# A linear-attention and token-mixing kernel: state kept as diagonal blocks, V loaded by whole batches, token sums on column halves, and a new order of steps

## The chip, the cores and the metric

The kernel runs on one core of a Trainium2 chip. The metric is device time in microseconds, as a median over executions. A core has five engines with queues of their own: TensorE (PE), VectorE (DVE), ScalarE (ACT), GpSimd (POOL) and SyncE (SP), which here issues almost all of the DMAs. [...]

## The reference

There are 4 batches, 8 heads, 768 tokens and 48 columns per head. The first part is a recurrence over the tokens; the second mixes tokens with a low rank and ends in a projection:

```python
for t in range(S):
    cur = einsum('bhd,bhe->bhde', u[None] * kt, vt)
    y[:, :, t] = einsum('bhd,bhde->bhe', rt, state + cur)
    state = wt[:, :, :, None] * state + einsum('bhd,bhe->bhde', kt, vt)
...
x = y.transpose(0, 2, 1, 3).reshape(B, S, H * D)          # 768 x 384 per batch
W_tok = scale * einsum('bsd,btd->bst', x @ w_q, x @ w_k)   # 64 columns each
out = maximum(einsum('bst,btd->bsd', W_tok, x), 0) @ w_out
```

Inputs and output are float32.

## The kernel before

**Tiling.** The work is cut into 12 units of 256 tokens, three to a batch, and each unit into two chunks of 128 tokens. Token pairs lie side by side in a row of a load, so each plain load moves runs of 384 bytes. The heads lie in four pairs; the two heads of a pair take 48 rows each of the two 64-row halves of the 128 partitions.

**A unit.** `load` brings w, k, r and v (one DMA each of 384 KB; tiles wg, kg, rg, vg, four buffers each). The logarithm of w (`f_ln`, tile lw) is summed over tokens by matmuls (`f_cw`), and `f_en`, `f_ep` take exponentials of both signs (tiles en, ep). K and R are cast to bf16 (`f_c16`, L475), transposed on TensorE (`f_rawT`), and multiplied with the exponentials: RT (`f_RT`, L536) and KT (`f_KT`, L547). Scores are matmuls of KT and RT with 48-row weights (`f_A`), masked on VectorE into AM (`f_am`, L619). The product of r, k and u gives one number per token and head (`f_dps`, `f_dd`), which scales V into Vd (`f_vd`, L601).

**State.** KT is transposed back (`f_kb`) and copied as kd (`f_kd`). In `f_sn` the outer products of kd and V are made by pairs of heads, so that 96 x 96 blocks hold the two heads' states on the diagonal and unused products beside it; four pairs make 384 columns. The state carried on is added by a matmul with an identity. `f_sb` (L666) decays it on VectorE by the tile ptm, which GpSimd makes (`f_ptm`) from ep and MB; MB holds zeros that clear the blocks off the diagonal. `f_y` adds, for one chunk, eight matmuls of AM and V and four of RT and the state SB.

**V.** For seven of the twelve units (`DIRECT`) `load_v` (L226) brings V with four DMAs of 192-byte runs to the rows in which it is needed, and one cast makes VB. For the other five a plain load is cast (tile v16), and `f_vp` moves its rows by matmuls with PM.

**The second part.** `f_x` (L707) makes X from y and Vd; `f_xt`, `f_qk` make the two projections (tile QK). After the third unit of a batch, `f_T` sums over all tokens of the batch: six matmuls of 384 columns, whose 128 weight columns are the 64 of a chunk and the 64 beside them; `f_Ts` copies 64 rows into a tile TS whose other rows are zero. Then per unit `f_mx`, `f_rl` (tile MX), `f_fp` and `f_os` make the output rows (tile os), and a DMA stores them.

**Order.** A planner (`Plan.order`) merges five queues, one per engine. The place of each step in its queue is written out in `RANK`; the engine of a step that could run on several is in `ENG`. The planner walks the queues with assumed durations and gives PSUM banks as it goes. [...] The 51 matmuls of zeros (tile Z) keep TensorE busy: nine at the start, 26 after the first unit's sums, 16 marked for the end.

**Set-up.** Before the first step VectorE clears the double buffers lw, r16, k16, kd, ts whole, GpSimd makes masks and identities (CM, PM, ID16, US), and ScalarE loads u.

Of the kernel before, what the change touches and what calls it, by code (L numbers as in the profile page):

```python
# [14 lines left out]
AX = mybir.AxisListType  # L15
# [9 lines left out]

class Plan:

    def __init__(self, kinds, switch):
        self.kinds = kinds
        self.switch = switch
        self.steps = []

    def add(self, eng, dur, rank, fn, after=(), fill=None, read=(), lag=100, mode=0,
            behind=None):
        s = dict(mode=mode, behind=behind, eng=eng, dur=dur, rank=rank, fn=fn, after=[a for a in after if a is not None],  # L40
                 fill=fill, lag=lag, n=len(self.steps), out=[])
        s["buf"] = None if fill is None else dict(readers=[])
        self.steps.append(s)
        for a in read:
            self.reads(s, a)
        return s

    def dma(self, issue, dur, rank, fn, after=(), fill=None, read=()):

        i = self.add("SP", issue, rank, fn, after, fill, read, lag=0)  # L50
        m = self.add("DQ", dur, 0, self.nothing, [i], lag=0)
        return i, self.add(f"L{m['n']}", 1950, 0, self.nothing, [m], lag=0)

    def nothing(self):
        pass

    def reads(self, s, a, own=False):

        if not own:
            s["after"].append(a)  # L60
        if a["buf"] is not None:
            a["buf"]["readers"].append(s)

    def order(self):
        never = 1 << 60
        queues = {e: [] for e in ("PE", "ACT", "DVE", "POOL", "SP")}
        for s in sorted(self.steps, key=lambda s: s["rank"]):
            if s["eng"] in queues:
                queues[s["eng"]].append(s)
            for a in s["after"]:  # L70
                a["out"].append(s)
        free = dict.fromkeys(queues, 0)
        free["DQ"] = 0
        place = dict.fromkeys(queues, 0)
        rings, owners, moved, done, mode = {}, [None] * 8, [], [], 0

        def clear(buf):

            if buf is None:
                return 0  # L80
            return max([x.get("end", never) for x in buf["readers"]], default=0)

        def start(s):

            if any("end" not in a for a in s["after"]):
                return never, None
            if s["behind"] is not None and "start" not in s["behind"]:
                return never, None
            t = max([free[s["eng"]]] + [a["end"] for a in s["after"]])
            if s["behind"] is not None:  # L90
                t = max(t, s["behind"]["start"])
            if s["eng"] == "SP" and len(moved) >= 3:
                t = max(t, moved[-3])
# [13 lines left out]
            if s["fill"] is not None:  # L107

                ring, size = rings.setdefault(s["fill"], []), self.kinds[s["fill"]]
# [9 lines left out]
        while True:  # L119
# [7 lines left out]
            if at is not None:  # L127
                s["buf"]["bank"] = at
# [4 lines left out]
            change = e == "PE" and s["mode"] != mode  # L133
            if e == "PE":
                mode = s["mode"]
            run(s, t, s["dur"] + self.switch * change)
            if e == "SP":
                for m in s["out"]:
                    if m["eng"] == "DQ":
                        run(m, max(free["DQ"], s["end"]), m["dur"])  # L140
                        moved.append(free["DQ"])
                        for x in m["out"]:
                            if x["eng"].startswith("L"):
                                run(x, m["end"], x["dur"])
        assert len(done) == len(self.steps)
        return done


@with_exitstack
def kernel(  # L150
# [24 lines left out]
    HW = H * D2  # L175

    SHIFT = 25
    MU = -SHIFT * math.log(2.0) / C

    def mm(o, l, rr, start=True, stop=True, trans=False):  # L180
        nc.tensor.matmul(o, l, rr, start=start, stop=stop,  # L181
                         skip_group_check=True, is_transpose=trans)
# [4 lines left out]
    sm = ctx.enter_context(tc.tile_pool(name="sm", bufs=3))  # L187
    bt = ctx.enter_context(tc.tile_pool(name="bt", bufs=2))
# [6 lines left out]
    NB = 4  # L195
    WG = [const([C, HW], F32, f"wg{i}") for i in range(NB)]
    RG = [const([C, HW], F32, f"rg{i}") for i in range(NB)]
    KG = [const([C, HW], F32, f"kg{i}") for i in range(NB)]
    VG = [const([C, HW], F32, f"vg{i}") for i in range(NB)]
    NOS = 4  # L200
    OS = [const([C, 2 * DM], F32, f"os{i}") for i in range(NOS)]
    EW = 132

    KDS = [const([C, 1024], BF16, f"kd{i}") for i in range(2)]
    LW = [const([C, 2 * H * 64], BF16, f"lw{i}") for i in range(2)]
    R16 = [const([C, 2 * H * 64], BF16, f"r16{i}") for i in range(2)]
    K16 = [const([C, 2 * H * 64], BF16, f"k16{i}") for i in range(2)]
    QK = [const([C, NU * 384], BF16, f"qk{i}") for i in range(2)]
    TS = [const([C, DM], BF16, f"ts{i}") for i in range(2)]
    EP = [const([C, 8 * EW], BF16, f"ep{i}") for i in range(2)]  # L210

# [8 lines left out]

    def load_v(b, i, tl):

        for c in range(2):
# [693 lines left out]
```

## Time and profile before

| what | us |
|---|---|
| median of three executions | 108.14 (107.78 to 108.36) |
| the profiled execution: span, first to last instruction | 105.2 |
| the profiled execution's own time | not on the page; the three executions lie 2.6 to 3.2 above the span |
| busy: PE / DVE / ACT / POOL | 96.2 / 88.1 / 79.9 / 71.0 |
| moved by DMA | 24.62 MB, 58,896 of 61,217 packets under 512 bytes |
| last load landed, last store landed | 82.30, 104.15 |

The granted TensorE clock is 1.000 in the whole span. A busy PE is modelled: its matmuls overlap, so the steps from start to start say more than its busy time. A line of a group reads: line, engine, operation, output <- inputs, shapes, count, then busy us and mean ns, then the idle time of the engine just before it. All matmuls go through one helper at L181, so they are told apart by their tiles.

### The profile page before, as it was taken

Reading aid. Unit: us, or ns where it says so; the run is one execution under the profiler, and the core shown is the slowest. Engines: PE = TensorE matmul, PEld = TensorE weight load, DVE = VectorE, ACT = ScalarE, POOL = GpSimd, SP = SyncE. Lnnn points to the kernel's source line nnn. Section 1 sums busy time; section 2 is a strip of 40 time slices with the busy share of each in tenths; the row PEclk is TensorE's granted clock in tenths of the full one; section 3 lists DMA queues with packets and bytes.
Section 4 is the critical chain, followed back from the end, with each engine's and each line's share of the span. In section 5 each row is a group of like instructions: output and inputs, shape, how many; then the busy total and the mean of one; then the engine's idle time right before and its main releaser. Section 6 shows DMA issues by size and latency. Waiting matters only on the chain.

```text
span 105.2 us, 3714 instructions
## 1 busy us (share of the span) xinstructions
PE 96.2 (91%) x1506; PEld 70.2 (67%) x1506; DVE 88.1 (84%) x138; ACT 79.9 (76%) x123; POOL 71.0 (67%) x92
## 2 busy tenths in 40 slices
PE   5969889997999998999997897779999999998995
PEld 2246566686887786968796775658697987856551
DVE  6898997898999999798999996786998889754740
ACT  4367778797989868997899959867898895954610
POOL 6600859599997996979979993968689699000000
DMA  1999999999999898989997969998997870033564
GB/s 28 298 324 325 325 323 270 238 297 175 312 316 264 148 272 230 288 172 310 325 311 142 213 123 269 350 289 209 288 255 143 303 307 18 0 153 150 199 243 160
DMA packets 61217, 24.62 MB, mean 234 GB/s; under 512 B 58896, under 2 KB 60048, under 8 KB 61200
## 3 DMA queue, kind: packets, MB, share of 16 engines
q1 hardware_dynamic: 60640, 24.19, 85.5%
q10 hardware_dynamic: 560, 0.20, 0.7%
q8 instruction: 11, 0.18, 0.7%
q14 instruction: 6, 0.05, 0.1%
HBM read 19.66 MB, written 4.72 MB: 232 GB/s over the span
## 4 chain that ended last, share of the span: by engine, by line
PE 51%; DVE 14%; DMA 13%; issue 7%; POOL 5%; ACT 4%; SPq 4%; DVEq 0%; ACTq 0%; POOLq 0%
PE PS L181 51%; DMA wg<-in_w_dram 7%; DMA kg<-in_k_dram 6%; SPq L226 3%; DVE SB L666 2%; DVE RT L536 2%; POOL KT L547 2%; DVE qT L529 2%; DVE KT L547 2%; POOL Vd L601 1%; ACT MX L381 1%; SPq L230 1%; ACT kd L373 1%; DVE X L707 1%; DVE kd L265 1%
## 5 line engine op out<-in xcount | busy, mean ns | idle before, releaser
L619 DVE TENSOR_TENSOR AM<-PS,US 128x1024 bf16<-128x1024 f32 x24 | 28.9, 1220 | 1.1 <-PE PS L181 0.7
L547 POOL TENSOR_TENSOR KT<-ks,en 128x1024 bf16<-128x1024 bf16 (+1 forms) x10 | 19.3, 1934 | 1.2 <-ACT en L498 0.6
L601 POOL TENSOR_TENSOR Vd<-VB,dd 128x768 bf16<-128x768 bf16 (+1 forms) x14 | 18.4, 1318 | 2.2 <-ACT dd L371 1.3
L181 PE MATMUL PS<-Z 128*128 128x512 bf16 x51 | 16.2, 424 | 1.5 <-DVE uT L248 1.2
L707 DVE SCALAR_TENSOR_TENSOR X<-PS,gx,Vd 128x768 bf16<-128x768 f32 (+1 forms) x13 | 12.3, 955 | 3.3 <-PE PS L181 2.8
L181 PEld LDWEIGHTS <-KT 48*128 48x128 bf16 (+1 forms) x272 | 10.7, 95 | 6.3 <-issue 3.8
L467 ACT ACTIVATE lw<-wg 128x768 bf16<-128x768 f32 x12 | 10.0, 846 | 5.5 <-DMA wg<-in_w_dram 5.1
L181 PE MATMUL PS<-wo,MX 128*128 128x384 bf16 x72 | 13.5, 326 | 0.1
L504 ACT ACTIVATE ep<-PS 128x1024 bf16<-128x1024 f32 (+1 forms) x14 | 12.7, 922 | 0.9 <-PE PS L181 0.9
L498 ACT ACTIVATE en<-PS 128x1024 bf16<-128x1024 f32 (+1 forms) x14 | 12.5, 904 | 0.5 <-issue 0.3
L666 DVE TENSOR_TENSOR SB<-PS,ptm 128x384 bf16<-128x384 f32 x20 | 11.1, 553 | 1.5 <-PE PS L181 1.3
L181 PE MATMUL PS<-RT,KT 48*128 48x128 bf16 x192 | 9.2, 217 | 1.4 <-POOL KT L547 0.5
L381 ACT ACTIVATE MX<-PS 128x768 bf16<-128x768 f32 (+1 forms) x12 | 8.7, 730 | 1.8 <-PE PS L181 1.7
L475 POOL CAST r<-rg 128x768 bf16<-128x768 f32 x10 | 8.7, 870 | 1.6 <-DMA rg<-in_r_dram 1.5
L475 POOL CAST k<-kg 128x768 bf16<-128x768 f32 x9 | 7.4, 825 | 3.3 <-DMA kg<-in_k_dram 2.0
L181 PE MATMUL PS<-ID,k 128*128 128x128 bf16 x96 | 7.4, 220 | 2.2 <-POOL k L475 1.4
L181 PEld LDWEIGHTS <-MX 128*128 128x128 bf16 x72 | 6.7, 98 | 3.9 <-issue 0.3
L373 ACT ACTIVATE kd<-PS,gv 128x384 bf16<-128x384 bf16 (+1 forms) x11 | 8.1, 740 | 1.4 <-PE PS L181 1.3
L181 PEld LDWEIGHTS <-Z 128*128 128x128 bf16 x51 | 5.0, 105 | 6.0 <-issue 2.3
L371 ACT COPY os<-PS 128x768 f32<-128x768 f32 (+1 forms) x10 | 7.1, 708 | 2.5 <-PE PS L181 2.2
L536 DVE TENSOR_TENSOR RT<-PS,ep 128x1024 bf16<-128x1024 bf16 (+1 forms) x14 | 8.4, 609 | 0.5 <-PE PS L181 0.2
L181 PE MATMUL PS<-CM,lw 64*128 64x128 bf16 x192 | 7.8, 223 | 1.1 <-ACT XT L371 0.7
(82 smaller groups left out, 211.4 us busy)
## 6 DMA issues: line engine op xcount, KB each, us to landing
wg<-in_w_dram SPq DMA_DIRECT2D x12, 384.0 KB, 5.3
kg<-in_k_dram SPq DMA_DIRECT2D x12, 384.0 KB, 5.0
rg<-in_r_dram SPq DMA_DIRECT2D x12, 384.0 KB, 5.1
out_dram<-os SPq DMA_DIRECT2D x9, 384.0 KB, 4.3
vg<-in_v_dram SPq DMA_DIRECT2D x28, 96.0 KB, 3.7
vg<-in_v_dram SPq DMA_DIRECT2D x5, 384.0 KB, 5.0
out_dram<-os SPq DMA_DIRECT2D x5, 192.0 KB, 2.0
wof<-in_moe_w_out_dram SPq DMA_DIRECT2D x1, 576.0 KB, 5.7
```

The source lines that it names most:

```text
L181: nc.tensor.matmul(o, l, rr, start=start, stop=stop, skip_group_check=True, is_transpose=trans)
L381: nc.scalar.activation(o, i, ACT.Relu)
L467: nc.scalar.activation(view(lw, 0, [[64, H], [512, 2], [1, D]]), view(wg, 0, [[D2, H], [D, 2], [1, D]]), ACT.Ln, bias=0.0, scale=math.exp( ...
L475: op(view(dst, 0, [[64, H], [512, 2], [1, D]]), view(src, 0, [[D2, H], [D, 2], [1, D]]))
L498: nc.scalar.activation(sb("en", [C, 1024])[:, cols(cs, 512)], t["cw"][:, cols(cs, 512)], ACT.Exp, bias=0.0, scale=-1.0)
L504: nc.scalar.activation(view(ep, cs[0] * NP * EW + 66, [[EW, NP * len(cs)], [-65, 2], [1, 64]]), t["cw"][:, cols(cs, 512)], ACT.Exp, bias=0 ...
L536: nc.vector.tensor_tensor(view(sb("RT", [C, 1024]), cs[0] * 512, [[C, n4], [64, 2], [1, 64]]), view(t["rT"], cs[0] * 512, [[C, n4], [64, 2 ...
L547: e.tensor_tensor(sb("KT", [C, 1024])[:, cols(cs, 512)], t["ks"][:, cols(cs, 512)], t["en"][:, cols(cs, 512)], ALU.mult)
L601: nc.gpsimd.tensor_tensor(sb("Vd", [C, 2 * DM])[:, cols(cs, DM)], t["VB"][:, cols(cs, DM)], view(t["dd"], cs[0] * H, [[1, len(cs) * H], [0 ...
L619: nc.vector.tensor_tensor(view(sb(f"AM{c}", [C, 1024]), 0, [[C, 8], [1, C]]), view(t[f"A{c}"], 0, [[C, 8], [1, C]]), view(US, 0, [[0, 8], ...
L666: nc.vector.tensor_tensor(view(x, 0, [[D, H], [1, D]]), view(t[f"sn{c}"], 0, [[D, H], [1, D]]), view(t["ptm"], c * 8, [[1, 8], [0, D]]), A ...
L707: nc.vector.scalar_tensor_tensor(view(X["t"], (2 * i + c0) * DM, [[DM, ncs], [1, DM]]), view(t["y"], c0 * 512, [[512, ncs], [1, DM]]), gx, ...
```

## The change

**State.** The state of the four pairs is kept in 192 columns: head 0 of a pair in rows 0 to 47, head 1 in rows 64 to 111, both in the same 48 columns. kd is laid out with a stride of 128 columns between zeros, so that a 128-column slice of it holds one head's columns at the right rows and zeros elsewhere. `f_sn` makes one matmul of 48 columns per head, and adds the carried state by a matmul with IDU, an identity scaled by 2 to the power -25; kd is scaled by the same number (gk). SB is decayed by ep directly; ptm and MB are gone.

**y.** Its part from the state comes first (`f_yi`), as matmuls with 48-row weights, one per head, in two sides; a side takes one head of a pair from chunk 0 and the other from chunk 1, and a drain of TensorE stands between the sides. The part from AM (`f_ya`) follows.

**V.** For batches 1 to 3 `load_whole` brings the V of the whole batch with four DMAs of 64 rows and 24 runs of 192 bytes per row, into two new buffers vw. VB is cast from it on GpSimd. Batch 0 uses plain loads and `f_vp`.

**Token sums.** In `f_T` chunk 0 of a unit goes to rows 0 to 63 of the PSUM tile and chunk 1 to rows 64 to 127, with 64 weight columns each; TS is copied with all 128 rows.

**Set-up.** Only the 16 pad columns of each 64 are cleared in lw, k16, r16; ts needs nothing; kd is cleared by GpSimd (2,112 columns, twice). The r cast of unit 0 goes to GpSimd.

**Order.** `RANK` is new, `ALT` picks the engine where there is a choice, and 17 movable matmuls of zeros all stand early. The order of the loads and stores on SyncE is new as well.

```diff
-    def load_v(b, i, tl):
-        for c in range(2):
-            src = v[b, :, ds(i * U + c * C, C)].rearrange("h (q j) d -> j q h d", j=2)
-            for j in range(2):
-                nc.sync.dma_start(out=view(tl, c * DM, [[D, H], [1, D]], p0=64 * j, pn=64),
-                                  in_=src[j])
+    def load_whole(b, q, tl):
+        n_ = H // 2 * NCH
+        for j in range(2):
+            nc.sync.dma_start(
+                out=view(tl, q * n_ * D, [[D, n_], [1, D]], p0=64 * j, pn=64),
+                in_=dataclasses.replace(v, offset=(b * H * S + j) * D + q * n_ * C * D,
+                                        ap=[[D2, 64], [C * D, n_], [1, D]]))
...
-    for t in R16 + K16 + KDS:
-        nc.vector.memset(t, 0.0)
+        for x in (tiles["lw"][0], tiles["k16"][0], tiles["r16"][0]):
+            nc.vector.memset(view(x, D, pads), 0.0)
...
+        for x in tiles["kd"]:
+            nc.gpsimd.memset(x, 0.0)
...
-                        mm(x[:, ds(0, DM)], ID16, old.tile, start=True, stop=False)
+                    mm(x[:, ds(0, NP * D)], IDU, old.tile, start=True, stop=False)
...
-                        mm(x[:, ds(hp * D2, D2)], KDS[n % 2][:, ds((c * NP + hp) * C, C)],
-                           t["VB"][:, ds(c * DM + hp * D2, D2)],
+                        mm(x[:, ds(hp * D, D)],
+                           kd.tile[:, ds(64 + (c * H + h) * 128 - 64 * hh, 128)],
+                           VB.tile[:, ds(c * DM + h * D, D)],
...
-                    nc.vector.tensor_tensor(view(x, 0, [[D, H], [1, D]]),
-                                            view(t[f"sn{c}"], 0, [[D, H], [1, D]]),
-                                            view(t["ptm"], c * 8, [[1, 8], [0, D]]), ALU.mult)
+                    view(SB.tile, 0, [[D, NP], [1, D]]), view(at(sn), 0, [[D, NP], [1, D]]),
+                    view(ep.tile, c * NP * EW + 64, [[EW, NP], [0, D]]), ALU.mult),
...
-                    for hp in range(NP):
-                        mm(y[:, ds(c * 512 + hp * D2, D2)], t["RT"][:, ds((c * NP + hp) * C, C)],
-                           old.tile[:, ds(hp * D2, D2)], start=False, stop=True)
+                if not first:
+                    nc.tensor.drain()
+                for hp in range(NP):
+                    for c, hh in side:
+                        mm(of(c, 2 * hp + hh), RT.tile[ds(hh * 64, D), ds((c * NP + hp) * C, C)],
+                           olds[c].tile[ds(hh * 64, D), ds(hp * D, D)],
+                           start=(first and hp == 0), stop=False)
...
-                    mm(batch["T"][:, ds(0, DM)], batch["QK"][:, ds(ii * 384 + c * DH, C)],
-                       X["t"][:, ds(gi_ * DM, DM)], start=(gi_ == 0), stop=(gi_ == NCH - 1))
+                mm(at(T)[ds(c * DH, DH), ds(0, DM)], QK.tile[:, ds(ii * QS + U + c * DH, DH)],
+                   X.tile[:, ds(gi * DM, DM)], start=(gi < 2), stop=(gi >= NCH - 2))
```

## The prediction

> **What bounds the kernel now.** I read the page's engine shares first, then busy time by stage, then the chain of waits, then the table of waits.
>
> ```profile
> PE 96.2 (91%) x1506; PEld 70.2 (67%) x1506; DVE 88.1 (84%) x138; ACT 79.9 (76%) x123; POOL 71.0 (67%) x92
> ```
>
> No engine stands alone, so the stages are asked (columns: stretch, length, busy us of PE, PEld, DVE, ACT, POOL, clock, DMA share, GB/s):
>
> ```profile
> 0.00:10.00 10.00, 7.94 (x55) 3.67 (x57) 7.98 (x27) 5.62 (x10) 3.53 (x20) 1.00 0.90 239
> 10.00:35.00 25.00, 23.34 (x421) 17.53 (x417) 23.29 (x32) 21.33 (x32) 20.67 (x24) 1.00 1.07 276
> 35.00:55.00 20.00, 19.49 (x348) 15.49 (x346) 18.38 (x26) 17.11 (x25) 17.80 (x19) 1.00 1.03 262
> 55.00:70.00 15.00, 12.42 (x239) 9.83 (x236) 12.96 (x18) 12.90 (x19) 12.08 (x13) 1.00 0.92 231
> 70.00:92.50 22.50, 21.96 (x383) 17.65 (x384) 19.87 (x28) 18.55 (x30) 16.89 (x19) 1.00 0.68 195
> 92.50:105.00 12.50, 11.00 (x76) 6.07 (x73) 5.57 (x11) 4.40 (x11) 0.00 (x0) 1.00 0.47 178
> ```
>
> Here is to be seen: from 10 to 35 us VectorE is 93% busy (PE's time there is padded with warm-up matmuls on Z); from 35 to 55 and from 70 to 92.5 TensorE is 97 to 98% busy; from 55 to 70 it loses 2.6 us while nobody is full. What holds it there is in the chain, in order of time:
>
> ```profile
> 59.09 1.58 SPq L226
> 60.72 0.72 SPq L226
> 61.48 0.62 SPq L230
> 62.22 0.58 SPq L230
> 63.30 6.31 DMA kg<-in_k_dram
> 69.66 0.84 POOL k L475
> 70.54 22.65 PE PS L181 x390
> ```
>
> SyncE issues two direct V loads of four DMAs each (L226), the K loads behind them go out late, and the cast of K starts when its load has landed. By the landing times, most loads of the kernel are used within 0.05 to 1.6 us of landing: they are just in time. From 70.5 us on the chain is TensorE without a break until 93 us. At the head, VectorE's memsets (groups of DVE until 8 us) run until 7.16 us, while unit 0's K landed at 5.92:
>
> ```profile
> L265 DVE MEMSET r<- 128x512 uint32 x2 | 1.0, 485 | 0.1
> L265 DVE MEMSET k<- 128x512 uint32 x2 | 1.0, 485 | 0.1
> L265 DVE MEMSET kd<- 128x512 uint32 x2 | 1.0, 485 | 0.1
> ```
>
> [...] a score matmul (48-row weights, 128 columns) that ends its group is followed after 148 ns, where 56 is the step inside a group, and the group before it pays the like (205 instead of 109, 139 instead of 42): some 95 ns each way. [...] 162 ns at 384 columns, 42 at 96, 25 at 48. [...] the half KT on VectorE took 0.43 us with GpSimd idle and 1.05 us beside a GpSimd cast. [...]
>
> **The change part by part.**
>
> *Head.* Off VectorE go 8 memsets of 485 ns (3.88), 2 of 218 for ts (0.44), 3 of 60 for MB (0.18) and the r cast (0.56). Added are 6 memsets of 128 words, 165 each by PM's row (1.0), IDU (0.11 to 0.28 by the rows of ID's memset and US) and gk (0.06). Net -3.8 us, so the k cast can start when K has landed: 1.24 us earlier. But GpSimd gets two memsets of 2,112 columns and the r cast (0.87). No row shows such a memset: at the price per column of GpSimd's cast (825/768 = 1.07 ns) it takes 2.26 us, at half of that, if two values go at once, 1.1. I take 2.0. GpSimd is free of its selects at 4.6, so r is cast by 4.6 + 4.0 + 0.19 (UB) + 0.87 = 9.7; transposes 0.67, RT 0.42, scores 0.40, and the first AM starts at 11.2 instead of 11.99: **-0.8** (-2.6 where the r load's landing at 6.98 binds, +0.2 at 2.26 a memset[...]).
>
> *State.* SB handles 192 columns instead of 384. From 1220 ns at 1024 and 553 at 384 columns the step is 1.04 ns, so 353: 20 times -0.20 = -4.0 us of VectorE. ptm goes from GpSimd (10 x 0.216 + 4 x 0.244 = -3.1). TensorE: outer products 80 x 42 become 160 x 25 (+0.6); the carried state 16 x (82 - 162) = -1.3; the part of y from the state 80 x 42 becomes 160 matmuls in 48-row tiles, 14 ns each if they pair as the scores do (3 ns, then one step), 25 if not: -1.1 to +0.6.
>
> *Token sums and V.* T: 24 x 162 becomes 12 pairs on column halves: -1.9 if they run together, 0 if not. Two fewer repack steps vp: 8 x 81 = -0.65, with two VB copies fewer on ScalarE (-1.6). VB for whole V is GpSimd's cast as before (9 + 3 instead of 7 + 5 casts of 0.82).
>
> *What TensorE pays.* Counted in the two instruction orders, it changes mode 83 times instead of 56: 27 x 0.095 = +2.6. The 13 drains between the two sides of y are not in this trace: 0 (the mode change covers it) to 158 ns (a 48-column matmul's 183 less its 25), I take 100: +1.3. TensorE's sum: +0.6 - 1.3 - 1.0 - 1.9 - 0.65 + 2.6 + 1.3 = -0.35, between -1.8 and +4.0. It is the whole of what is bound by TensorE, at 42.5 of 105 us: **-0.2**.
>
> *Order and engines.* By counts times rows VectorE loses 5.1 us in all, ScalarE 4.9, GpSimd (KT: one full and one half more, +3.3; ptm -3.1) nothing outside the set-up. From 10 to 35 us VectorE sheds KT of units 0, 1 and 3 (2.6, half of unit 0 stays on it) and 0.2 for each of 6 SB, and takes two ks (1.4), a cast (0.56) and a kd (0.4): -1.4. GpSimd takes those KTs and is then full: by its own durations without idle time KT of unit 4 ends at 31.7 instead of 34.5. I take **-0.9** (-2.5 to +1.5).
>
> *Loads.* V in 192-byte runs goes from 7 to 9 units: by packet times 4,096 x 16.7 ns less 2,048 x 22.8, over 16 engines, +1.4 us of transfer. But SyncE issues 12 large V DMAs instead of 28 small of 0.63 us, and a whole V (batch 2's after unit 7's loads, batch 3's after unit 10's) finds a buffer that was freed long before, where a V of one unit now waits for GpSimd's casts. Unit 11's K and W come last, behind two stores; by ScalarE's order and durations the second store's copy is done at 57 us without idle time, some 63 with its present share, so they land near 70, before 72.67 and 73.86 of now. The weights move behind six loads and V: some 38 instead of 25 us, ahead of their first use. I take **-2.3** of the 2.6 lost at 55 to 70 us (-2.6 to +1). ScalarE's gain lies under its 5.1 us of waiting for W: 0. What is late next is GpSimd: its VB of unit 3 waits for the first whole V, due near 34 us (20 loads by 27.4, then 6 to 7.5), and casts, Vd and the weights queue behind; TensorE's y of unit 3 waits for it.
>
> *Tail.* From the end of the last X (92.42) to its last output matmul (100.84) TensorE has 6.9 us of matmuls for 8.4 us; two output blocks of batch 2 (0.98 each) now lie there to fill the rest: **-0.5**. The 15 warm-ups that go from the end cost nothing: the last ended at 104.07, and the last store landed at 104.15.
>
> Sum: -0.8 - 0.2 - 0.9 - 2.3 - 0.5 = -4.7, so a span of 100.5 against 105.2. The median of the runs shown is 108.14, 2.9 above this span (the page gives no other time of the profiled execution); I carry the 2.9 over: **103.4 us**.
>
> **The rivals.**
>
> *Loads set the pace (17%).* For it: slacks of 0.1 us after landing and a DMA share near 1 until 80 us. Against it: 7 us or so of its time are gaps in which SyncE waited for buffers. Then +1.4 stays, the head gives 0.8 and the tail 0.5 back: 108.2.
>
> *TensorE becomes slower (15%).* Its place is y and T: mode changes at 95 ns each, 13 drains at 158, no pairing in y, no pairing in T: +4.0 in the sum above, all of it on the path where engines are as closely matched as from 35 to 92 us, and the order's gain at 55 to 70 us goes to it. 108.14 + 4.0 - 0.8 - 0.5 = 110.8. It decides from the point where TensorE's sum is above +4.5, or above +2.2 if the loads give nothing. For it: 97 to 98% in two stages. Against it: the scores do pair.
>
> *The order fits better than the sum says (10%).* GpSimd, never idle, would end its last Vd at 78.6 instead of 89.5; if three quarters of these 10.9 us reach the end, the span is 97.0 and the time 99.9.
>
> *The forecast (58%)*: 101.0 to 106.2.
>
> **How the numbers follow.** About 0.5% is what a measurement of this kernel can tell from no change: 107.6 to 108.7. Faster holds the forecast, the last case and a fifth of the loads case, less 2%: 0.70. The same: half of the loads case and the forecast's edge: 0.10. Slower: the rest, 0.20. The range runs from 100.0 to 109.0: half of the last case and most of the slow one lie outside.
>
> **What will show it.** Right: first AM near 11.2 us; SB at 353 ns; GpSimd's kd memsets near 2 us; y's state part with steps of 3 and about 25 ns; T in 12 steps of 162; the wait for K near 63 us gone; VectorE's sum near 83. Wrong: GpSimd waiting at VB of unit 3 for more than 3 us; TensorE's idle time between 35 and 92 us above today's; a last K or W landing after 74 us.

## The result, and the profile after

The changed kernel takes **113.39 us** (median of four, 112.17 to 114.45); the kernel before, beside it, 107.96. The ratio is **1.0485 [1.0376, 1.0595]**: slower by about 5 us, where 103.4 us with a range of 100.0 to 109.0 was predicted. A time is the median of all executions, while a ratio leaves out the slow ones of both kernels, so that the two do not divide exactly. The profiled execution is the longest of the four: 114.45 us, at a span of 112.7.

First the shares of the engines, from the page of the changed kernel:

```profile
PE 93.3 (83%) x1633; PEld 69.8 (62%) x1633; DVE 85.2 (76%) x138; ACT 76.1 (68%) x114; POOL 74.8 (66%) x82
```

TensorE, VectorE and ScalarE are all busy for less time than before (96.2, 88.1, 79.9), and the span is 7.5 us longer. For TensorE that is the matmuls of zeros: they take 16.2 us of its busy time before and 8.9 now, so its own work rose from 80.0 to 84.4 us. No engine became the bound of the whole; all of them wait more. By stage (stretch, length, busy us of PE, PEld, DVE, ACT, POOL, granted clock, DMA share, GB/s), still of the changed kernel:

```profile
0.00:10.00 10.00, 7.16 (x40) 2.71 (x40) 5.10 (x20) 5.21 (x9) 8.16 (x23) 1.00 0.91 238
10.00:35.00 25.00, 21.38 (x406) 16.43 (x407) 22.54 (x32) 18.25 (x23) 21.49 (x19) 0.93 1.10 260
35.00:55.00 20.00, 17.19 (x355) 14.14 (x356) 15.82 (x25) 14.61 (x23) 14.30 (x14) 0.91 1.05 252
55.00:70.00 15.00, 12.69 (x236) 9.89 (x235) 11.33 (x18) 10.80 (x15) 11.40 (x12) 1.00 0.93 233
70.00:92.50 22.50, 19.88 (x397) 15.76 (x396) 18.41 (x27) 17.39 (x27) 17.37 (x15) 1.00 0.71 162
```

From 35 to 92.5 us TensorE is busy for 49.8 us; before it was 53.9 in the same stretches. The one column that stays near 1 until 70 us is the DMA share. The chain of waits of the changed kernel says the same (start, length, what):

```profile
32.08 5.78 DMA vw0x<-in_v_dram
...
38.41 0.83 POOL VB1x L543
...
52.10 6.83 DMA vw1x<-in_v_dram
...
59.80 0.83 POOL VB1x L543
...
67.92 0.93 SPq L291
68.91 1.09 SPq L298
...
73.53 5.74 DMA vw0x<-in_v_dram
79.53 0.67 issue
80.20 2.12 POOL KT0x L532
...
84.40 0.83 POOL k161x L458
...
96.30 11.54 PE PS L239 x122
```

Where before had K and then TensorE, there are now three whole V (L298), one for each batch from 1 to 3, with steps of GpSimd behind each: its cast VB after the first two, KT after the third. The table of GpSimd's waits in the changed kernel (us in total, times, longest) has them on top:

```profile
POOL VB1x L543 <- DMA vw0x<-in_v_dram: 6.0, 2, 3.5
POOL r160x L458 <- DMA rg0x<-in_r_dram: 2.4, 2, 1.8
...
POOL k161x L458 <- DMA kg3x<-in_k_dram: 2.1, 2, 1.3
```

It is tempting to stop here: "GpSimd waits for V". The experiments show that taking most of this wait away gains nothing. What the changed kernel loses, and where, can be seen in the units' progress. The start of each unit's X (us), read from the traces; the last two rows are kernels of the experiments:

| unit | 0 | 1 | 2 | 3 | 4 | 5 | 6 | 7 | 8 | 9 | 10 | 11 |
|---|---|---|---|---|---|---|---|---|---|---|---|---|
| before | 18.0 | 24.1 | 30.1 | 38.3 | 44.7 | 55.3 | 60.0 | 67.6 | 73.3 | 82.5 | 86.7 | 91.3 |
| changed | 23.7 | 28.8 | 32.3 | 44.4 | 51.5 | 56.3 | 65.5 | 72.5 | 77.3 | 90.2 | 94.9 | 97.1 |
| a_replan | 15.8 | 23.6 | 32.6 | 41.5 | 47.4 | 52.7 | 63.5 | 71.4 | 75.7 | 85.1 | 92.8 | 93.7 |
| a_replan_m2 | 18.7 | 23.5 | 30.9 | 37.4 | 45.7 | 52.1 | 59.8 | 63.6 | 70.8 | 80.7 | 86.0 | 89.4 |

And the landings, where the changed kernel's loads fall behind (us; from the DMA issues in the traces):

| | W, unit 8 | W, unit 9 | W, unit 11 | K, unit 11 | last input |
|---|---|---|---|---|---|
| before | 54.8 | 55.9 | 72.7 | 73.9 | 82.3 (V, unit 11) |
| changed | 60.6 | 69.0 | 85.6 | 84.4 | 85.6 (W, unit 11) |

The last input comes only 3.3 us later, but it is another one: before it was V of the last unit, which is needed last; now it is W, with which the unit begins.

### The profile page after: what moved, and what is told of

The parts are those of the page before. It is cut to its first block, busy times and chain, and to the rows that moved or that the text cites. A ratio compares the mean times of both kernels' runs of the same rounds, so it can differ in the third digit from the quotient of the medians.

```text
span 112.7 us, 3924 instructions
## 1 busy us (share of the span) xinstructions
PE 93.3 (83%) x1633; PEld 69.8 (62%) x1633; DVE 85.2 (76%) x138; ACT 76.1 (68%) x114; POOL 74.8 (66%) x82
## 4 chain that ended last, share of the span: by engine, by line
PE 34%; POOL 19%; DMA 16%; SPq 12%; issue 9%; ACT 4%; DVE 2%; POOLq 0%; DVEq 0%; ACTq 0%
PE PS L239 34%; DMA vw0x<-in_v_dram 10%; SPq L298 9%; DMA vw1x<-in_v_dram 6%; POOL Vd0x L581 3%; SPq L291 2%; POOL KT0x L532 2%; POOL kd1x L350 2%; POOL VB1x L543 1%; POOL VB0x L543 1%; POOL r160x L458 1%; POOL k161x L458 1%; POOL r161x L458 1%; POOL k160x L458 1%; POOL Vd1x L581 1%
## 5 line engine op out<-in xcount | busy, mean ns | idle before, releaser
L532 POOL TENSOR_TENSOR KT0x<-ks0x,en0x 128x1024 bf16<-128x1024 bf16 (+1 forms) x6 | 11.8, 1963 | 1.9 <-ACT en0x L489 1.9
L532 POOL TENSOR_TENSOR KT1x<-ks1x,en1x 128x1024 bf16<-128x1024 bf16 (+1 forms) x6 | 10.8, 1805 | 1.8 <-DVE dd0x L386 0.9
L581 POOL TENSOR_TENSOR Vd1x<-VB1x,dd1x 128x768 bf16<-128x768 bf16 (+1 forms) x7 | 9.3, 1338 | 2.2 <-ACT dd1x L380 2.2
L239 PE MATMUL PS<-Z 128*128 128x512 bf16 x26 | 8.9, 484 | 1.2 <-DVE uT L308 1.2
L581 POOL TENSOR_TENSOR Vd0x<-VB0x,dd0x 128x768 bf16<-128x768 bf16 (+1 forms) x7 | 9.0, 1292 | 0.4 <-ACT dd0x L380 0.3
L601 DVE TENSOR_TENSOR AM00x<-PS,US 128x1024 bf16<-128x1024 f32 x6 | 7.3, 1222 | 0.8 <-PE PS L239 0.6
L601 DVE TENSOR_TENSOR AM01x<-PS,US 128x1024 bf16<-128x1024 f32 x6 | 7.3, 1223 | 0.7 <-PE PS L239 0.6
L601 DVE TENSOR_TENSOR AM11x<-PS,US 128x1024 bf16<-128x1024 f32 x6 | 7.3, 1219 | 0.1
L601 DVE TENSOR_TENSOR AM10x<-PS,US 128x1024 bf16<-128x1024 f32 x6 | 7.3, 1219 | 0.1
L484 ACT ACTIVATE ep0x<-PS 128x1024 bf16<-128x1024 f32 (+1 forms) x7 | 6.5, 921 | 0.1
```

Source lines behind the costliest of these rows:

```text
L239: return nc.tensor.matmul(o, l, rr, start=start, stop=stop, skip_group_check=True, is_transpose=trans)
L484: nc.scalar.activation(view(ep.tile, cs[0] * NP * EW + 66, [[EW, NP * len(cs)], [-65, 2], [1, 64]]), at(cw)[:, ds(cs[0] * 512, w_)], ACT.E ...
L532: x.tensor_tensor(KT.tile[:, cols], ks.tile[:, cols], en.tile[:, cols], ALU.mult)
L581: nc.gpsimd.tensor_tensor(Vd.tile[:, cols], VB.tile[:, cols], view(dd.tile, cs[0] * H, [[1, len(cs) * H], [0, D]]), ALU.mult)
L601: AMs[c] = add(("AM", n, c), {"D": 1221}, lambda e, c=c, A=A: nc.vector.tensor_tensor(view(AM[c].tile, 0, [[C, 8], [1, C]]), view(at(A), 0 ...
```

## The experiments

Each ratio is the time over that of the kernel before in the same session. Line numbers of the kernels `a_...` are some 35 lower than in the changed kernel.

**1. V in thirds, and V without the wait.** In `a_v_unit` each unit's V is a transfer of its own; in `a_v_nowait` everything is transferred as in the changed kernel, but VB of batches 2 and 3 reads what landed a batch earlier.

```diff
a_v_unit
-            batch["vwL"] = [plan.dma(("vw", n, q), 1500, 2930, ... load_whole(b, q, x) ...) for q in range(2)]
+            batch["vwL"] = [plan.dma(("vt", n), 2500, 1950, ... load_third(b, i, x) ...)]
a_v_nowait
-                view(batch["vw"].tile, 2 * i * D, ...)), batch["vwL"], VB, [batch["vw"]])
+                view(batch["of"].tile, 2 * i * D, ...)), batch["vwL"] if b == 1 else [], VB, [batch["of"]])
```

> The changed kernel, but V of batches 1 to 3 is loaded unit by unit (four DMAs of 64 rows each, at the place of the whole V for units 3, 6 and 9, two or three loads later for the others); casts, engines and the order of all other steps as they were. Theory V (the whole V lands late, GpSimd waits for it, SyncE's loads wait for GpSimd): VB of units 3, 6 and 9 start 3 us or more earlier, unit 11's K and W land before 80 us, and the time falls by 4 to 7 us, from 113.4 to 106.5-109.5. Theory drains (TensorE pays for drains and mode changes): VB may start earlier, but the time stays above 111.5. Theory order (the new step order itself is worse): above 111.5 too.

> The changed kernel with the same transfers in the same order, but the casts of V of batches 2 and 3 read the V of the batch before, which landed long ago (so V of a wrong batch is used); only batch 1 waits for its whole V. Theory V-wait (GpSimd's wait for the whole V is what costs): the waits of 6 us ahead of VB of units 6 and 9 go, and the time falls by 4 us or more, to 109.4 or less. Theory loads (the transfer queue is never idle until the last input has landed, and the order of loads and steps is laid for faster transfers): K, R and W of the later units land when they did, so the time stays within 1.5 us of 113.4.

Measured: `a_v_unit` 114.28 us, 1.0743 [1.0647, 1.0840]; `a_v_nowait` 113.72 us, 1.0530 [1.0355, 1.0704]. In the first, V of unit 3 landed at 33.7 instead of 37.9 and V of unit 9 at 76.0 instead of 79.3, but W of unit 6 came at 46.6 instead of 44.3. In the second, GpSimd's waits for V fell to the first one:

```profile
POOL VB1x L511 <- DMA vw0x<-in_v_dram: 4.3, 1, 4.3
...
POOL k161x L426 <- DMA kg3x<-in_k_dram: 2.9, 2, 2.2
```

VB of unit 9 started at 75.3 instead of 79.4, and yet X of unit 9 at 89.3 (90.2) and X of unit 11 at the same 97: K of unit 11 landed at 81.1 and W at 84.0. Theory V-wait falls for batches 2 and 3; the wait of batch 1, which stands ahead of X of unit 3, was left in. `a_v_unit` moved that one too: V of unit 3 came 4.2 us earlier and X of unit 3 3.3 us earlier (41.0), and no time was gained; VB of units 6 and 9 started within 0.3 us of where it did. `a_v_unit` alone would not have shown that, since its four DMAs for each unit also put the other loads back.

**2. Whole V alone, in the order of before.**

```diff
+                if i == 0:
+                    issue, land = plan.dma(3000, 5860, ..., lambda: load_whole(b, VW[b % 2]), fill="vw")
```

> The kernel before with this part of the change alone: V of batches 1 to 3 loaded whole at the place in SyncE's order where V of units 3, 6 and 9 was, and cast by GpSimd; all other steps in their old order (vp and the ScalarE copy of units 3, 6 and 9 go, 3 x 0.33 us of TensorE and 3 x 0.8 us of ScalarE). Theory V: VB of unit 3 starts at 36 us or later (32.9 now), and the time is 110 to 114 instead of 108.0. Theory drains or order: 107 to 109, since this part is harmless in the old order.

Measured: 112.58 us, 1.0576 [1.0460, 1.0693]. One line of its table of GpSimd's waits:

```profile
POOL VB L555 <- DMA vw<-in_v_dram: 5.8, 1, 5.8
```

W of unit 5, which stands behind the whole V, landed at 37.5 instead of 32.7, and X of unit 3 started at 45.1 instead of 38.3. In an order that is not made for it, whole V costs as much as the entire change. Wait and displaced loads are not separated here, nor is the TensorE clock, which is at half in this trace for 6.8 us from 36.9 on, and at full speed throughout in the trace of before.

**3. Lighter loads.** From unit 4 on, two of the eight heads of r, k and w are not loaded.

```diff
+        h_ = H if b * NU + i < 4 or ap is v else 6
...
-            out=view(tl, 0, [[D2, H], [1, D2]]), in_=ap[b, :, ds(i * U, U)]...
+            out=view(tl, 0, [[D2, h_], [1, D2]]), in_=ap[b, ds(0, h_), ds(i * U, U)]...
```

> The changed kernel, but from unit 4 on the loads of r, k and w bring 6 of 8 heads (the last two heads then hold older data); nothing else differs. That takes 24 x 0.25 x 1.2 = 7.2 us of transfer off the queue. Theory loads (the new order runs ahead of what the loads can bring, so the loads set the pace of the whole kernel): the time falls by 5 us or more, from 113.4 to 105-108.5. Theory drains and theory order (TensorE's drains and mode changes, or the engines' order in itself): it stays above 111.5.

> The kernel before with the same lighter loads (6 of 8 heads of r, k and w from unit 4 on). Theory loads: the order before leaves the loads just in time but not in the lead, so it gains at most 1.5 us (106 to 108). If it gains as much as the changed kernel, both are paced by loads alike, and something else makes the difference.

Measured: changed 106.46 us, 0.9915 [0.9838, 0.9993]; before 104.30 us, 0.9689 [0.9575, 0.9802]. By the ratios that is 6.2 us off the changed kernel ((1.0485 - 0.9915) x 108) and 3.4 us off the kernel before. So loads pace both, contrary to the 1.5 us expected for before, and the changed kernel nearly twice as much. Two stages of the changed kernel with lighter loads show TensorE full again:

```profile
55.00:70.00 15.00, 14.51 (x297) 12.03 (x296) 13.68 (x21) 13.32 (x19) 14.06 (x13) 1.00 1.07 234
70.00:92.50 22.50, 21.99 (x441) 17.88 (x440) 19.32 (x30) 17.89 (x30) 14.32 (x14) 1.00 0.36 125
```

**4. Drains in the changed kernel.** The matmuls write to PSUM (PS in the traces), where the y of a unit has two banks, one for each chunk. `a_nodrain` gives each half of the heads one of them and leaves 11 of the 13 drains out; no run leaves them out with the banks as they were. `a_drain2` does the opposite and doubles each drain.

```diff
a_nodrain
-            return at(ys[c])[:, ds((0 if end else c * 512) + h * D, n_ * D)]
+            return at(ys[c])[:, ds(h * D if end else hh * 512 + c * 192 + hp * D, n_ * D)]
-            sides = [[(0, 0), (1, 1)], [(1, 0), (0, 1)]]
+            sides = [[(0, 0), (0, 1), (1, 0), (1, 1)]]
a_drain2
                     nc.tensor.drain()
+                    nc.tensor.drain()
```

> The changed kernel, but each y has one PSUM bank for each half of the heads instead of one for each chunk[...]: 11 of the 13 drains go, the two steps of y's state part become one in 11 units, and X is made by two VectorE instructions instead of one in these (about +0.2 us each, 2.2 us in all). Theory V: the time stays within 1.5 us of 113.4, since the waits for V set the end. Theory drains: 11 x 0.265 = 2.9 us and some mode changes go, less a part of VectorE's 2.2: 109.5 to 111.5.

> The changed kernel with two drains in a row where it has one. Theory drains (each drain's bubble of some 0.265 us is on the path): if the second costs as much as the first, 13 x 0.265 = +3.4 us, to 116.8; if a second drain of an empty TensorE is nearly free, +0 to 1. Theory V: at most +1.5 even where each bubble grows by 0.1 us or more, since most of y's work waits for V anyway.

> The changed kernel with the lighter loads (6 of 8 heads of r, k and w from unit 4 on) and with a PSUM bank for each half of the heads, so without 11 of the 13 drains. The lighter loads alone gave 106.5, and from 56 us on their chain is TensorE. Theory drains: where TensorE sets the end, the drains after 56 us (6 x 0.265 = 1.6 us) and some of those before come back, 104 to 105.2. If the drains are hidden there too: 106 to 107.

(`a_light_nd` has the edit of `a_nodrain` and the lighter loads of 3.)

Measured: `a_nodrain` 112.25 us, 1.0440 [1.0300, 1.0580]; `a_drain2` 112.70 us, 1.0561 [1.0437, 1.0686]; `a_light_nd` 107.17 us, with times from 105.04 to 108.08, too far apart for a ratio: inconclusive. In the trace of `a_drain2` the second drain adds 80 ns to a bubble of 271, so `a_drain2` adds only 1.0 us to TensorE in all and can't price the first. In the changed kernel no cost of the drains is seen, with intervals of more than 1% on either side; 7 and 9 show a cost elsewhere.

**5. The set-up.** kd is cleared as words, in two steps of GpSimd that stand behind the first casts.

```diff
-        for x in tiles["kd"]:
-            nc.gpsimd.memset(x, 0.0)
+    kdz = [add(("kdz", x), {"P": 1150}, lambda e, x=x: nc.gpsimd.memset(
+        tiles["kd"][x].bitcast(I32), 0)) for x in range(2)]
```

> The changed kernel with the two memsets of kd out of GpSimd's set-up: done as 1,056 words each, the first after unit 0's r cast, the second after unit 1's. Theory head (the set-up's end on GpSimd sets the start of everything): the r cast of unit 0 starts near 7.1 us instead of 9.4, the first AM near 10.3, and the time falls by 1.5 to 2.3 us. Theory loads: the first AM comes earlier all the same, but the time stays within 0.7 us, since the loads of later units land when they did.

Measured: 112.78 us, 1.0473 [1.0363, 1.0583]. The first AM came at 10.5 instead of 12.6, and X of unit 0 at 23.9 instead of 23.7. Two microseconds won at the head are gone before the first unit is done. What X of unit 0 stands behind is in VectorE's timeline of the changed kernel (start, length):

```profile
21.92 1.89 DVE L458 CAST r161x<-rg3x 128x768 bf16<-128x768 f32 x1
23.73 1.00 DVE L705 SCALAR_TENSOR_TENSOR X0x<-PS,gx,Vd0x 128x768 bf16<-128x768 f32 x1
```

The cast of R of unit **3** is ahead of X of unit 0 in VectorE's queue, and that R landed at 21.8 in the changed kernel and at 21.7 in `a_head`. In the changed kernel the last matmul of unit 0's y ends at 21.7, so this cast holds X for 2.0 us. In `a_head` y ends at 20.5, VectorE then sits idle for R, and X is held for 3.4 us:

```profile
21.82 2.13 DVE L422 CAST r161x<-rg3x 128x768 bf16<-128x768 f32 x1 [1.27 <-DMA rg3x<-in_r_dram]
```

**6. The same steps in another order, some of them on other engines.** The order of the changed kernel comes with a planner whose durations are shorter than those of before: a load 1,190 ns where it was 1,440. In the trace of the changed kernel the landings of r, k and w lie 1.55 us apart on average (34 from 6 to 88 us, each from the landing before it), and a half of a whole V takes 3.0 us. I searched for another order with the kernel's own planner, with durations as measured. They served the search alone; what differs in the kernel is the table of places and engines (its numbers are left out here):

```diff
-RANK = [...]
-ALT = "..."
+KEYS = {...}
...
-        e = next(iter(engs)) if len(engs) == 1 else next(self.alt, "")
-        e = e if e in engs else next(iter(engs))
+        e = KEYS[key][0] if key in KEYS else next(iter(engs))
...
-        for s_, x in zip(plan.steps, RANK):
-            s_["rank"] = x
+    for s_ in plan.steps:
+        s_["rank"] = KEYS[s_["key"]][1] if s_["key"] in KEYS else 0
```

> The changed kernel, instruction for instruction, in another order of steps on the five engines (and other choices between the engines where the code has a choice): found by a search in the kernel's own planner with a load at 1,440 ns instead of its 1,190, half a whole V at 3,200 instead of 2,930, a drain at 265 instead of 60, GpSimd's set-up at 9,000 instead of 6,500 ns and a store at 1,400 instead of 960. Theory order (the changed order is laid for loads faster than the chip brings them): the time falls by 3 us or more, to 107-110.4. Theory parts (whole V, drains and mode changes cost what they cost in any order): 112 or more.

> As the last, but with V of batches 1 to 3 in thirds (one unit each, each placed by the search), a PSUM bank for each half of the heads (11 drains fewer, X in two instructions) and the two memsets of kd later. Theory whole V (what is left after the order is that K, R and W of the next units stand behind three units' V): 104 to 107, 3 us or more under the re-ordered kernel with whole V. If V's form doesn't matter, within 1.5 us of that one.

Measured: `a_replan` 109.92 us, 1.0199 [1.0054, 1.0344]; `a_replan_v` 109.43 us, 1.0182 [1.0054, 1.0311]. By the ratios the new order is worth 2.9% with the same steps. It is not order alone: VectorE, ScalarE and GpSimd now run 143, 118 and 73 instructions, where they ran 138, 114 and 82, and the order of the loads differs too. X of unit 0 in the timeline of `a_replan`:

```profile
15.13 0.66 DVE L422 CAST r161x<-rg1x 128x768 bf16<-128x768 f32 x1
15.76 1.02 DVE L669 SCALAR_TENSOR_TENSOR X0x<-PS,gx,Vd0x 128x768 bf16<-128x768 f32 x1
```

Now the cast ahead of it is of unit 1, and X of unit 0 starts 8 us earlier; W of unit 11 lands at 79.7. Thirds of V brought nothing: their 36 small DMAs took 22.4 us of the queue (each landing counted from the one before it), the 12 of whole V 18.1 in the changed kernel, and the last input of `a_replan_v` landed at 87.2.

**7. The other parts alone, in the order and with the loads of before.**

```diff
-    for t in R16 + K16 + KDS:
-        nc.vector.memset(t, 0.0)
+    for t in LW + R16 + K16:
+        nc.vector.memset(view(t, D, [[64, 16], [1, 16]]), 0.0)
...
-                    mm(y[:, ds(c * 512 + hp * D2, D2)], t["RT"][:, ds((c * NP + hp) * C, C)], ...
+                    for hh in range(2):
+                        if hh:
+                            nc.tensor.drain()
+                        for hp in range(NP):
+                            mm(y[:, ds(c * 512 + (2 * hp + hh) * D, D)], ...
...
-                    mm(batch["T"][:, ds(0, DM)], batch["QK"][:, ds(ii * 384 + c * DH, C)], ...
+                    mm(batch["T"][ds(c * DH, DH), ds(0, DM)], batch["QK"][:, ds(ii * 384 + c * DH, DH)], ...
```

> The kernel before, in its old order of steps and with its old loads, with the other parts of the change: state as diagonal blocks in 192 columns (20 drains here, one in each y with a state part, since a y of this order is one step for each chunk), token sums on column halves, pads instead of whole memsets (VectorE zeroes kd here). Theory loads and order: what engines save or pay is covered by the loads, so the time stays within 1.5 us of before (106.4 to 109.4). Theory parts: 20 x 0.265 = 5.3 us of drains and 40 mode changes of 0.095 = 3.8 us against 4 us saved on VectorE and 3 on TensorE make it slower by 2 us or more, 110 to 114.

> As b_parts, with a PSUM bank for each half of the heads in all units but the last: 2 drains are left of 20, X is made by two instructions of VectorE in 11 units. Theory parts: 18 x 0.265 = 4.8 us of drains go, less up to 2.2 us on VectorE: 2 us or more under b_parts. Theory loads and order: within 1 us of b_parts, and a gain on before of at most 1.5 us.

Measured: `b_parts` 113.36 us, 1.0433 [1.0346, 1.0520]; `b_parts_nd` 110.65 us, 1.0152 [1.0100, 1.0203]. The engine shares of the two pages, `b_parts` first:

```profile
PE 102.7 (92%) x1659; PEld 74.8 (67%) x1666; DVE 82.0 (74%) x135; ACT 80.4 (72%) x123; POOL 68.2 (61%) x78
```

```profile
PE 98.3 (90%) x1659; PEld 71.0 (65%) x1666; DVE 83.7 (77%) x146; ACT 81.1 (74%) x123; POOL 68.4 (63%) x78
```

Here theory parts wins: VectorE is busy for 6 us less and TensorE for 6.5 more, and TensorE is what the old order is tight on (97 to 98% busy in two stages of before). One of the four executions of `b_parts` had the full clock throughout and took 113.23 us; the others took 113.23 to 114.16. The first AM starts at 10.4 instead of 12.0 us, so the set-up keeps its promise when VectorE clears kd, but X of unit 2 is already late (32.8 for 30.1). The 20 drains lengthen the step from one matmul's start to the next by 0.235 us each, 4.7 us in all; without 18 of them the time is 2.8% (3 us) lower.

**8. V contiguous for six units, and a control.** The re-ordered kernel without 11 drains gets V of units 0 to 3, 6 and 9 by one contiguous load each and a turn on TensorE, the others by four DMAs. `b_replan` is the kernel before after the same search.

```diff
-    WHOLE = (1, 2, 3)
+    DIRECT = (4, 5, 7, 8, 10, 11)
```

> The changed kernel's parts (without 11 drains, memsets of kd later) in an order found by the planner's search with measured durations (a load 1,440 ns, a V of four small DMAs 2,350), and V as before's kernel loads it: units 4, 5, 7, 8, 10 and 11 by four DMAs, the other six in one contiguous load and turned by TensorE. Theory V's transfers (three units' V cost 6.1 us whole and 7.5 us in thirds, 3.6 us contiguous): the last input lands before 84 us and the time is 106 to 108. If V's form doesn't matter: 109 to 110, as the two re-ordered kernels before.

> The kernel before, instruction for instruction, in an order that the same search found with the same measured durations (a load 1,460 ns, a V of four small DMAs 2,500). Theory search (an order found for the real transfers is what gains): 1 to 3% faster than before, as the re-ordered changed kernel with contiguous V (0.980). Theory parts (the parts of the change gain once their order fits): within 0.7% of before.

> The changed kernel's parts with V of six units contiguous and without 11 drains, as the run before of that form, with a longer search at the durations of b_replan. Theory search: the same as b_replan within 1%. Theory parts: 1% or more faster than b_replan, 0.96 to 0.98 of before.

Measured: `a_replan_m` 108.11 us, **0.9801 [0.9748, 0.9854]**; `b_replan` 109.38 us, 1.0138 [1.0078, 1.0198]; `a_replan_m2` 104.87 us, **0.9721 [0.9651, 0.9791]**. The search brought the kernel before nothing, which speaks for the parts of the change: they gain with an order and with loads that fit. As a control it has two weak points. It left every step of before on its engine, where the search for the changed kernel chose engines too; and `b_replan` ran with TensorE at half clock from 7.6 to 14.4 us. TensorE is busy for 5.18 us of that stretch, so by an estimate up to 2.6 us are due to the clock, and 106.8 us would still be above `a_replan_m2`. `a_replan_m` does not tell V's form from its other differences to `a_replan_v`, and its last input landed at 89, against what was expected; in `a_replan_m2` it landed at 79.9. Nor did V itself get cheaper in sum: each landing counted from the one before it, all V take 20.5 us of the queue in before, 21.7 in the changed kernel and 22.8 in `a_replan_m2`. The chain of `a_replan_m2` has TensorE for 30 us on end, from earlier than the 70.5 us of before:

```profile
56.02 30.45 PE PS L203 x613
```

**9. The drains once more, in the fastest form.**

```diff
-            sides = [[(0, 0), (0, 1), (1, 0), (1, 1)]]
+            sides = [[(0, 0), (1, 1)], [(1, 0), (0, 1)]]
```

> The fastest form (a_replan_m2) with one PSUM bank for each chunk again: 11 drains are back, each y's state part is two steps with a drain between them at the place of the one step, and X is one instruction of VectorE again. Theory drains (TensorE is on the path from 57 us on): 11 x 0.265 = 2.9 us, less up to 2.2 us that VectorE gets back: 105.5 to 107.8. If both hide: within 0.6 us of a_best.

> a_replan_m2 once more, to be compared with a_m2_drain on the same chip: 104.5 to 105.3, 0.965 to 0.979 of before.

Measured: `a_m2_drain` 107.20 us, 0.9976 [0.9917, 1.0035]; `a_best` 106.81 us, 0.9776 [0.9683, 0.9869], less of a gain than in its first measurement (0.9721); the two intervals overlap. This ratio rests on two of six executions (104.47 and 105.66 us); over all of them the median is 1.3% under that of the kernel before. By the ratios 11 drains, with X in one instruction, cost 2.0%, 2.2 us: with them the fastest form only equals the kernel before.

## Why the prediction was wrong

**Loads: -2.3 was predicted, and the sign was wrong.** The step that failed is the reading of SyncE's waits as gaps in the transfers ("7 us or so of its time are gaps in which SyncE waited for buffers"). SyncE did wait, but the queue behind it was not empty: by the packets of both traces there is no moment from 10 to 80 us in which none is under way, and fewer than eight are for only 3 of these 70 us. The stage table of the prediction had it, with DMA shares of 1.07, 1.03 and 0.92. In such a queue a V that is brought earlier puts a K, R or W back: in `a_v_unit` V of unit 3 landed 4.2 us earlier and W of unit 6 2.3 us later. The first whole V landed at 37.9 (34 said, since 20 loads were taken to land by 27.4; they landed by 31.4), W of unit 11 at 85.6 (70 said). That the changed order let W and K of the last unit come last was seen, and priced as a gain. The two stores ahead of them were expected to be free at 57 to 63 us; ScalarE's copy for the second ended at 70.6, and SyncE came to them only after the whole V of batch 3. From SyncE's timeline of the changed kernel:

```profile
75.10 2.44 SPq L817 DMA_DIRECT2D out_dram<-os0x  x1
78.03 0.36 SPq L817 DMA_DIRECT2D out_dram<-os1x  x1
78.44 0.46 SPq L291 DMA_DIRECT2D kg3x<-in_k_dram  x1
78.95 0.84 SPq L291 DMA_DIRECT2D wg3x<-in_w_dram  x1
```

Of the rival "loads set the pace" the mechanism was right and the size wrong: it had +1.4 us of transfer and nothing for the order of the landings.

**Order: -0.9, and the tail -0.5.** Counted was what each engine sheds in a stage, not what stands behind what. X of unit 0 starts 5.7 us later than before, and VectorE's queue would have shown a part of it: R of unit 3 ahead of X, 2.0 us. By X of unit 2 the delay is down to 2.2 us; the one that lasts, 6.1 us, comes with X of unit 3 behind the first whole V. `a_replan` prices order and choice of engines at 2.9%. The tail from the end of the last X to the last output matmul is 8.9 us (98.96 to 107.83), not the 7.9 said: the two output blocks of batch 2 that lie there were added to it, they did not fill it (TensorE is busy for 8.9 us there, for 7.9 us of 8.4 before). That the order failed because of the planner's short durations is argued, not shown: no search was made with 1,190.

**TensorE: -0.2.** Most terms came out: the scores' pairing holds for y (3 ns, then 22 to 25), T takes three pairs for each batch, 159 to 184 ns apart, SB 0.35 us for 0.353. The prediction's 162, 42 and 25 ns at 384, 96 and 48 columns are steps from start to start in the trace of before. A mode change is the prediction's word for a change between 48-row and 128-row weights, which cost some 95 ns there; these changes were not measured apart. Against the sum of -0.35 us TensorE's own busy time rose by 4.4 us, with what drains and clock add to it. The drain was mis-sized: 100 ns, with bounds of 0 and 158. The 13 drains lengthen the step from start to start by 236 to 273 ns, 3.43 us in all instead of 1.3. The share carried over was rounded up: 0.35 x 42.5 / 105 is 0.14, not 0.2. Four matmuls of one side and four of the next in TensorE's timeline of the changed kernel (start, length):

```profile
95.95 0.27 PE L239 MATMUL PS<-SB2x,RT1x 48*128 48x48 bf16 x4
96.30 0.27 PE L239 MATMUL PS<-SB3x,RT1x 48*128 48x48 bf16 x4
```

A side's four starts take 0.1 us, and the next side starts 0.35 us after the first. The bound from above was a 48-column matmul's duration less its step, and every one of the 13 drains cost more. What this costs depends on what paces the stage: nothing clear of the noise in the changed kernel, 3 us for 18 of them in the old order, 2.2 us for 11 in the fastest form.

**Head: -0.8.** The memsets of kd were sized rightly (4.0 said, 4.1 measured), but the first AM came at 12.56, not 11.2. GpSimd reached the memsets 0.5 us later than said, so r of unit 0 was cast at 10.2 instead of 9.7. From there to AM it took 2.4 us instead of 1.5: four matmuls of zeros and the sums of unit 1 stood ahead of the scores on TensorE. VectorE's k cast of unit 0 ran beside the memsets and took 1.57 us, not 0.56, but KT's first half was ready at 9.3, so this did not hold AM up. Groups of the changed kernel (busy us, mean ns):

```profile
L350 POOL MEMSET kd1x<- 128x2112 bf16 x1 | 2.3, 2268 | 0.0
L350 POOL MEMSET kd0x<- 128x2112 bf16 x1 | 1.9, 1857 | 0.1
L458 DVE CAST k160x<-kg0x 128x768 bf16<-128x768 f32 x1 | 1.6, 1566 | 1.7 <-DMA kg0x<-in_k_dram 1.7
```

In the trace of before GpSimd was idle at this cast (0.56 us). The half KT of the prediction, too, took longer beside a step of GpSimd (1.05 us for 0.43); why is not shown. The head decided nothing: `a_head` won the two microseconds and lost them again.

**The rivals were taken as exclusive.** "Loads set the pace" moves the loads' term from -2.3 to +1.4, "TensorE becomes slower" moves TensorE's from -0.2 to +4.0. Both can happen together: 103.4 + 3.7 + 4.2 = 111.3, out of the range. That this is near the result is in part luck: TensorE's +4.0 was not measured (y and T paired after all), and the sum has nothing for the order or for the clock.

**The clock stands in no term.** The prediction carried over the full clock of before without a word. In the trace of the changed kernel TensorE has half its clock in two stretches, and is busy almost throughout (columns as in the table by stage):

```profile
26.30:29.70 3.40, 3.32 (x56) 2.84 (x53) 2.57 (x5) 2.48 (x3) 3.40 (x4) 0.50 0.99 241
40.00:43.40 3.40, 3.24 (x48) 2.96 (x48) 2.98 (x5) 1.04 (x1) 3.40 (x4) 0.50 1.11 313
```

Matmuls of 128 columns start 106 to 107 ns apart there, and 56 ns apart elsewhere. If all of these 6.56 us had taken half as long, 3.3 us would have been saved: an estimate from above of what the clock can have cost directly, and too much to leave out of 5 us. It does not explain the gains of the experiments: `a_replan` has two such stretches too and is 2.9% faster, and `a_light` has one and is 5.7% faster.

The three signs named for a wrong prediction were the right ones, and all three came: GpSimd waited 3.5 us at VB of unit 3, TensorE was idle for 7.7 us instead of 3.6 between 35 and 92.5 us, and the last W landed after 74.

**What the parts are worth.** In the old order whole V alone costs 5.8% and the other parts alone 4.3%; all together in their own order 4.9%. If the two costs simply add, that order takes back about half of them; no run shows that they do. Another order takes back 2.9% more, and contiguous V and fewer drains with an order for them end 2.0 to 2.8% under the kernel before by the ratios. **`a_replan_m2` beats both kernels.**

**Still open:** how much of b_whole's loss is the wait and how much the loads behind V; and what the granted clock costs, and why it fell. No run took the clock alone. Within one kernel the two go together: of the 22 executions of `a_m2_drain`, the seven with a mean clock of 0.99 or more took 106.2 us on average, the 13 near 0.98 took 107.6 and the two near 0.967 took 109.2. Which of the two comes first is not shown, and in `a_replan` the link is not seen (109.53 us at 0.999, 110.31 and 108.95 at 0.96 and 0.97).

## What to carry to other kernels

Where the transfer queue never runs empty, as here, read the landings in their order: an operand that is fetched early puts another back (V 4.2 us earlier, W 2.3 us later in `a_v_unit`). An order written for assumed durations should be held against the measured spacing of landings, and a part judged in the order that fits it: the parts without most of their drains cost 1.5% in the old order, and with an order and loads made for them the kernel gains 2.0 to 2.8%. Rival causes that can happen together should be summed for the range, and a clock that is full before is not bound to stay so (1.000 in the trace of before, 0.965 in that of the changed kernel).

## What had not been expected of the hardware

- A drain of TensorE between two groups of matmuls lengthened the step from start to start by 235 to 273 ns (13 drains of the changed kernel, 20 of `b_parts`); a second one right behind it added 80 (`a_drain2`).
- Three units' V took 3.5 us in contiguous loads of 384 bytes a run (1.18 each), 6.0 in the four DMAs of a whole V, 7.5 in twelve DMAs by units, the last two in runs of 192 bytes: by sums of landings in the changed kernel and in `a_replan_v`.
- GpSimd's memset of 2,112 bf16 columns took 1.9 and 2.3 us, and 0.97 to 0.98 us as 1,056 words (in `a_head`).
- TensorE's clock fell to half for 3.4 or 6.8 us at a time in most traces of the experiments (14 of 18 have a mean granted clock of 0.94 to 0.985), with 106 to 107 ns between matmuls of 128 columns instead of 56 (changed kernel, `b_replan`); in the trace of before it did not.
